# A Fourier mixer on one core: the setup and the first batch in another order, the fold of U on GpSimd, U's columns of the first batch in a pass of their own, and two of its four channel pieces moved into the loop

## The chip, the core and the metric

The kernel runs on one core of a Trainium2 chip. A core has five engines with a queue each, and every queue is worked in order: TensorE (PE; its weight loads are listed apart as PEld), VectorE (DVE), ScalarE (ACT), GpSimd (POOL) and SyncE (SP, which only issues transfers). The metric is the device time of one execution in microseconds (us); less is better. Times below that look like "at 47.2" are us from the first instruction of the profiled execution.

## The reference

`x` has shape 8 x 3136 x 256 (batch, sequence, channel) in float32. Without its casts the reference is:

```python
X = np.fft.fft(np.fft.fft(x, axis=1), axis=2).real   # along the sequence, then along the channels
h = X.transpose(0, 2, 1) @ U @ V                     # U 3136x32, V 32x3136
u = X + h.transpose(0, 2, 1)
out = u + np.maximum(u @ w_ch1, 0) @ w_ch2           # 256x1024 and 1024x256
```

So each batch has a two-dimensional Fourier transform of which the real part is kept, a low-rank mixing along the sequence, and a two-layer product over the channels. The last is most of the work: 49 chunks of 512 rows.

## The kernel before

**Tables.** The kernel makes its cosine and sine tables itself. `iota` on POOL gives the frequencies (`krow`, `kev`, `ncol`) and the row numbers for the gathers (`xidx`); DVE turns them into phases (`phase`, L180 and L182), ACT into sines (`sine`, L187; `cosine_even`, L604 and L606). By symmetry most of the tables follow from a quarter of them: `mirror_even` and `cosine_odd` copy with a sign on ACT, `other_even` and `other_odd` multiply by a row of alternating signs (`srow`) on DVE, and `halve` (L310, L312) halves one row with a scalar per partition. `TABE`, `TABO` and `TABS` hold the tables for even, odd and half-odd rows. `MSN` and `MC` are the sine and cosine of the channel transform; row 0 of `MSN` is overwritten with +1 and -1 by two memsets on POOL (`msr`, L687 and L688), so that it carries the two lone channels.

**U.** The low-rank factor U is transformed once. `fold_u` (L206 to L223) adds and subtracts forward rows `UF` and reversed rows `UR`; `transform_u(t)` gives three steps for t = 0 (sine) and t = 1 (cosine): `even_k` and `odd_k`, 36 small matmuls (L256) together, and `evict`, five ACT copies (L298 to L304) into spare columns of the tables. From then on, each group of matmuls of a batch's sequence transform also gives 32 columns of the product with U (`tab`).

**A batch.** `x` is loaded twice, forward by four indirect gathers on POOL (`load_f`, into `xf`) and reversed by SP (`load_r`, into `xr`); `load_0` brings the few rows that fall outside. DVE folds: `along_d` (L350 subtracts, L352 adds channels d and 256-d, in bf16), `alone` (the two channels without a partner), `mirror` (forward against reversed rows, L360 and L363), `half` (L368) and `fourth` (L372). The results `GO` and `GC` are the weights of the sequence transform. `seq(b, par, typ, pn)` is one group of matmuls (L427) for odd or even outputs (`par`), sine or cosine side (`typ`), first or second half (`pn`); the first half is copied to `ev` by ACT (L432) and for odd outputs turned into `eh` by DVE (L435, L437), and after the second half DVE joins both into `A` or `B` (L452 to L462). The join of the odd sine group is followed by a change of sign on POOL (L465). `chan(b, ch, h)` transforms one of four pieces along the channels for one of two halves (L473 with `MC`, L475 with `MSN`), and ACT copies it to `S` or `T` (L477). `lowrank` multiplies `tab` with `MDT` (L485) into `TA` and then makes a mirrored row of `VA` from `S` and `T` on DVE (L489). `VA` holds V in its first 32 rows, that mirrored row, and zeros.

**A chunk.** `front(c)` multiplies `TA` with `VA` (L511) and DVE adds it to `S` or `T`, giving `u` (L519); `first_product` multiplies with W1 (L531) and ACT applies the ReLU (L533); `second_product` multiplies with W2 (L547) and DVE adds `u` (L553 to L556) before the result is stored.

**What sets the order.** Up to `front(0)` the instructions of each engine run in the order in which the program lists them (`manual_schedule`, closed by `order.close()`). There the first batch is folded by columns: first all that the sine side needs (columns 0 to 128 and 256, 257), then the cosine side (128 to 256). A one-element transfer `gate` (L692) makes SP wait for batch 0's forward rows before it loads batch 1. After that a planner orders each engine's work; the listing gives its order of preference, and `due` spreads the steps of batch b (`transform(b)`: 8 fold steps, 8 groups, 8 channel pieces, `lowrank`) over the chunks of batch b-1.

Of the kernel before, what the change touches and what calls it, by code (L numbers as in the profile page):

```python
# [16 lines left out]
P = 128  # L17
PQ = 98
KP = PQ + 1
# [12 lines left out]
def kernel(  # L32
# [87 lines left out]
    load_0(x, xf, xr, 0, D)  # L120
    for q0 in (1, 0):
        load_r(x, xr, 0, q0, 2, D)
    iota(kev[:, 0:NT], [[-2, 2], [-4, NT // 2]], 392)
    iota(kev[:, NT:2 * NT], [[-2, NT]], 391)
# [40 lines left out]
    srow = cpool.tile([KP, 2 * NT], BF16, name="srow")  # L165
# [31 lines left out]
    phe = gen.tile([KP, 2, 2 * NT], I32, name="phe", bufs=1)  # L197
    uy = cpool.tile([KP, 2, 2, 2, NI * R], FP32, name="uy")
# [7 lines left out]
    def fold_u():  # L206
        for t in range(2):
            op = AL.add if t else AL.subtract
            nc.vector.tensor_tensor(uy[:, t, 0].rearrange("p a (i r) -> p a i r", r=R),
                                    UF[:, 0:4:2], UR[:, 3::-2, ::-1], op=op)  # L210
            nc.vector.tensor_tensor(uy[:, t, 1].rearrange("p a (i r) -> p a i r", r=R),
                                    UR[:, 0:4:2, ::-1], UF[:, 3::-2], op=op)
        nc.vector.tensor_tensor(GUO.rearrange("p t n i r -> p (t n) (i r)"),  # L213
                                uy.rearrange("p t n a x -> p (t n) a x")[:, :, 0],
                                uy.rearrange("p t n a x -> p (t n) a x")[:, :, 1], op=AL.subtract)
        nc.vector.tensor_tensor(ueven.rearrange("p t n x -> p (t n) x"),
                                uy.rearrange("p t n a x -> p (t n) a x")[:, :, 0],
                                uy.rearrange("p t n a x -> p (t n) a x")[:, :, 1], op=AL.add)
        for c in range(2):
            nc.vector.tensor_tensor(GUC[c].rearrange("p t i r -> p t (i r)"), ueven[:, :, 0],  # L220
                                    ueven[:, :, 1], op=AL.add if c == 0 else AL.subtract)
            nc.vector.tensor_single_scalar(NUC[c][:], GUC[c][:, :, 2, :], -1.0, op=AL.mult)
            nc.vector.tensor_single_scalar(NUO[:, :, c, :], GUO[:, :, c, 2 - 2 * c, :], -1.0, op=AL.mult)  # L223
# [27 lines left out]
    def transform_u(t):  # L251
# [22 lines left out]
        def even_k():  # L274
            pu = PU[t] = psum.tile([P, 16, R], FP32, tag="dft", name="pu", bufs=3)
# [49 lines left out]
    def cosine_odd(i):  # L325

        sgn = 1.0 if i == 0 else -1.0
        nc.scalar.activation(both(1, i, 1, 0, 1, NT), both(0, i, NT - 1, NT - 1, -1, NT),
                             AF.Copy, scale=sgn)
        nc.scalar.activation(TABO[1][:, 0, i // 2, 0:2 * NT], TABO[0][:, 0, i // 2, 2 * NT - 1::-1][:, 0:2 * NT],  # L330
                             AF.Copy, scale=sgn)

    def other_odd(t):

        nc.vector.tensor_tensor(TABO[t][:, 1, :, 0:2 * NT], TABO[1 - t][:, 0, :, 0:2 * NT],
                                strip(srow[:], 0, [[0, 2], [1, 2 * NT]]), op=AL.mult)

    def other_even(t):

        def cells(u, nm):  # L340
            v = TABS[u][:, nm, 0, :]
            return bass.AP(v.tensor, v.offset + off_t(u, 1),
                           [v.ap[0], [WS + off_t(u, 3) - off_t(u, 1), 2], [1, NT]])
        nc.vector.tensor_tensor(cells(t, 1), cells(1 - t, 0),
                                strip(srow[:], 0, [[0, 2], [1, NT]]), op=AL.mult)
# [8 lines left out]
    def alone(qs, src, dst):  # L354

        nc.gpsimd.tensor_copy(dst[:, qs, :, 128:257:128], src[:, qs, :, 0:129:128])
# [36 lines left out]
    def seq(b, par, typ, pn):  # L393
# [8 lines left out]
        d = ST[b]  # L402
        pt = psum.tile([P, QW], FP32, tag="dft", name="pt", bufs=3)
        mm = []

        def add(t, col, odd):

            if par == 0:
                for c in range(2):
                    g = GC[b % 2][0 if (c == 0) == (t == 1) else 1]  # L410
                    lo, hi, at = ((0, TE - NT + NE, 0), (TE - NT + NE, WE, TE - NT))[c]
                    for i in ((0, 2) if odd else (1, 3)):
                        mm.append((at, g[:kp(i), i, col:col + P], TABE[t][:kp(i), i, lo:hi]))
            else:
                for i in ((0, 2) if odd else (1, 3)):
                    at = 0 if odd else NT * slot(t, i)
                    tab = TABO[t] if odd else TABS[t]
                    for nm in range(2):
                        mm.append((at, GO[b % 2][:kp(i), nm, i, col:col + P],
                                   tab[:kp(i), nm, i // 2, :]))  # L420
        if typ == 1:
            add(1, 128, pn == 1)
        else:
            add(0, 0, pn == 1)
            add(1, 256, (pn == 1) == (par == 1))
        for n, (at, w, rhs) in enumerate(mm):
            nc.tensor.matmul(pt[:, at:at + rhs.shape[-1]], w, rhs, start=(n == 0),  # L427
                             stop=(n == len(mm) - 1), skip_group_check=True)
        if pn == 0:
            ev = d["ev"] = wp.tile([P, QW], FP32, tag="ev", name="ev", bufs=2)  # L430
            w = WO if par else QW
            nc.scalar.copy(ev[:, :w], pt[:, :w])  # L432
            if par == 1:
                eh = d["eh"] = wp.tile([P, 2 * NT], FP32, tag="eh", name="eh", bufs=2)
                nc.vector.tensor_tensor(eh[:, 0:NT], ev[:, NT - 1::-1], ev[:, WO - 1:WS - 1:-1],  # L435
                                        op=AL.subtract)
# [314 lines left out]
```

## Time and profile before

| what | value |
|---|---|
| median of 3 runs | 490.25 us (489.94 to 490.83) |
| the profiled execution's own time | 490.67 us |
| its span, first to last instruction | 488.9 us |
| PE busy | 449.7 us (92% of the span) |
| DVE busy | 342.7 us (70%) |
| ACT busy | 273.3 us (56%) |
| POOL busy | 88.1 us (18%) |
| HBM read and written | 29.26 MB and 25.69 MB |
| first matmul of U's transform | at 19.3 us |
| first group of batch 0 on PE | at 31.2 us |
| first channel piece of batch 0 | at 47.2 us |
| first `u` of chunk 0 on DVE | at 54.1 us |
| first group of batch 1 on PE | at 73.1 us |

Busy shares are averages over a beginning, in which the tables and the first batch are made, and a long loop. In the page's slices each digit is the busy share of one fortieth of the span in tenths. The chain of waits lists the work that ended last, followed back from the end; in order of time its lines give start, length, engine, what was written, and the line. A group of instructions is given with its shortest, median and longest duration in ns. A timeline line gives start, length, engine, line, operation, output and inputs with their shape, and in brackets how long the engine idled before and what released it.

### The profile page before, as it was taken

How to read it: one execution, taken by the hardware profiler on the slowest of the kernel's cores; microseconds unless marked ns; L12 is line 12 of the kernel's file. 1: busy time of each engine (PE TensorE's matmuls, PEld its weight loads, DVE VectorE, ACT ScalarE, POOL GpSimd, SP SyncE). 2: the span in 40 equal slices, each digit the busy share in tenths (PEclk: the TensorE clock that was granted, in tenths of full speed). 3: DMA queues.
4: the chain of work that ended last, by engine and by line, in shares of the span. 5: the costliest groups of instructions: out<-in, count | busy, mean ns of one | idle time of the engine just before them, and what ended most of it. 6: DMA issues, size and time to landing. Idle time of an engine off the chain costs nothing.

```text
span 488.9 us, 8177 instructions
## 1 busy us (share of the span) xinstructions
PE 449.7 (92%) x3096; PEld 299.9 (61%) x3096; DVE 342.7 (70%) x771; ACT 273.3 (56%) x533; POOL 88.1 (18%) x109
## 2 busy tenths in 40 slices
PE   0364799999999999999999999999999999999997
PEld 0342267666766666666766676666766676666665
DVE  5999699999999999997984358343743374434333
ACT  5331655665557554765566655756466556656562
POOL 7745230424144321610010001000010001000000
PEclk9997899999999999999999999999999999999999
DMA  5778389499839995595232422334223352333433
GB/s 149 157 135 236 64 152 254 134 253 260 231 89 220 245 249 163 134 272 142 70 104 65 131 67 68 102 89 129 67 66 86 108 88 86 88 98 99 128 90 126
DMA packets 87275, 67.14 MB, mean 137 GB/s; under 512 B 53920, under 2 KB 80556, under 8 KB 87236
## 3 DMA queue, kind: packets, MB, share of 16 engines
q1 hardware_dynamic: 81588, 51.86, 41.2%
q0 software_dynamic: 5648, 14.76, 11.8%
q8 instruction: 24, 0.39, 0.3%
q14 instruction: 15, 0.12, 0.1%
HBM read 29.26 MB, written 25.69 MB: 112 GB/s over the span
## 4 chain that ended last, share of the span: by engine, by line
PE 79%; DVE 16%; issue 2%; POOL 1%; ACT 1%; DVEq 0%; POOLq 0%
PE p L547 32%; PE p L531 31%; PE pt L427 6%; PE ph L511 4%; PE pst L473 3%; PE pst L475 2%; DVE eof L352 1%; DVE B L452 1%; DVE eof L350 1%; DVE u L519 1%; DVE eor L350 1%; DVE eor L352 1%; DVE A L452 1%; DVE B L456 1%; POOL uf L56 1%
## 5 line engine op out<-in xcount | busy, mean ns | idle before, releaser
L533 ACT ACTIVATE h<-p 128x512 bf16<-128x512 f32 x392 | 218.5, 597 | 139.6 <-PE p L531 139.4
L531 PE MATMUL p<-u,w 128*128 128x512 bf16 x784 | 210.1, 379 | 2.7 <-DVE u L519 2.7
L547 PE MATMUL p<-w,h 128*128 128x256 bf16 x1568 | 203.7, 273 | 0.0
L547 PEld LDWEIGHTS <-h 128*128 128x128 bf16 x1568 | 153.1, 98 | 59.2 <-DVE o L556 0.3
L531 PEld LDWEIGHTS <-w 128*128 128x128 bf16 x784 | 75.5, 98 | 59.8 <-issue 3.8
L553 DVE TENSOR_TENSOR o<-p,ut 128x4 f32<-128x4 f32 (+1 forms) x100 | 16.1, 161 | 111.3 <-PE p L547 111.2
L56 POOL DMA_INDIRECT xf<-in_x_dram,xidx x32 | 40.2, 1257 | 72.8 <-DVE eof L352 51.4
L465 POOL TENSOR_SCALAR B<-B 1x392 bf16<-1x392 bf16 x8 | 14.6, 1823 | 181.9 <-DVE tab L462 129.7
L556 DVE TENSOR_TENSOR o<-p,ut 128x254 f32<-128x254 f32 (+1 forms) x100 | 40.5, 405 | 0.0
L555 DVE TENSOR_TENSOR o<-p,ut 128x254 f32<-128x254 f32 (+1 forms) x100 | 40.5, 405 | 0.0
L519 DVE TENSOR_TENSOR u<-ph,S 128x512 bf16<-128x512 f32 (+15 forms) x64 | 34.9, 554 | 0.1
L432 ACT COPY ev<-pt 128x424 f32<-128x424 f32 (+1 forms) x32 | 16.4, 513 | 32.9 <-PE pt L427 21.4
L519 DVE TENSOR_TENSOR u<-ph,T 128x512 bf16<-128x512 f32 (+15 forms) x64 | 34.8, 553 | 0.0
L427 PEld LDWEIGHTS <-go 98*128 98x128 bf16 x192 | 19.4, 102 | 18.9 <-DVE go L368 7.1
L511 PE MATMUL ph<-va,ta 128*128 128x512 bf16 (+18 forms) x128 | 29.7, 329 | 0.5 <-ACT ta L488 0.5
L427 PE MATMUL pt<-te,gc 98*128 98x229 bf16 (+1 forms) x192 | 24.8, 268 | 0.3 <-DVE tab L459 0.2
L473 PE MATMUL pst<-A,mc 128*128 128x392 bf16 (+1 forms) x64 | 22.7, 355 | 2.3 <-DVE A L452 1.4
L427 PE MATMUL pt<-to,go 98*128 98x424 bf16 x96 | 21.8, 367 | 2.6 <-DVE tab L462 2.6
L475 PE MATMUL pst<-B,msn 128*128 128x392 bf16 (+1 forms) x64 | 22.7, 354 | 0.0
L427 PEld LDWEIGHTS <-gc 98*128 98x128 bf16 x192 | 18.6, 100 | 6.4 <-DVE tab L459 2.8
L477 ACT CAST S<-pst 128x392 bf16<-128x392 f32 (+1 forms) x32 | 15.7, 489 | 12.1 <-PE pst L475 12.1
L256 PE MATMUL pu<-guo,ts 99*98 99x32 bf16 (+1 forms) x16 | 2.3, 239 | 19.3 <-DVE guo L213 19.3
(120 smaller groups left out, 364.1 us busy)
## 6 DMA issues: line engine op xcount, KB each, us to landing
out_dram<-o SPq DMA_DIRECT2D x48, 512.0 KB
xr<-in_x_dram SPq DMA_DIRECT2D x7, 1568.0 KB
xr<-in_x_dram SPq DMA_DIRECT2D x2, 784.0 KB
ut<-u SPq DMA_TRANSPOSE x49
xf<-in_x_dram,xidx POOLq DMA_INDIRECT x32, 6.6
w<-in_moe_w_ch_dram POOLq DMA_DIRECT2D x1, 512.0 KB, 7.8
out_dram<-o SPq DMA_DIRECT2D x4, 128.0 KB
va<-in_moe_V_dram POOLq DMA_DIRECT2D x2, 196.0 KB, 5.2
```

Of the source, the lines that this page charges most:

```text
L56: nc.gpsimd.indirect_dma_start(out_, None, bass.AP(t.tensor, t.offset, [[w, rows], [1, w]]), bass.IndirectOffsetOnAxis(idx, 0), element_of ...
L427: nc.tensor.matmul(pt[:, at:at + rhs.shape[-1]], w, rhs, start=(n == 0), stop=(n == len(mm) - 1), skip_group_check=True)
L432: nc.scalar.copy(ev[:, :w], pt[:, :w])
L473: nc.tensor.matmul(pt[:, :hi - lo], MC[:, h * P:(h + 1) * P], d["A"][:, lo:hi], start=True, stop=False)
L475: nc.tensor.matmul(pt[:, :hi - lo], MSN[:, h * P:(h + 1) * P], d["B"][:, lo:hi], start=False, stop=True)
L511: nc.tensor.matmul(ph[:, col:col + hi - lo], TA[b % 2][:, s * P:(s + 1) * P], VA[b % 2][:, lo:hi], start=True, stop=True)
L519: nc.vector.tensor_tensor(u[:, s, col:col + hi - lo], ph[:, col:col + hi - lo], src, op=AL.add)
L531: nc.tensor.matmul(p1[:], W1[:, s, j * P:(j + 1) * P], k["u"][:, s, :], start=(s == 0), stop=(s == 1))
L533: nc.scalar.activation(k["h"][:, j, :], p1[:], AF.Relu)
L547: nc.tensor.matmul(p2[:, t % w, :], h[:, j, rs], W2[:, j, :], start=(j == 0), stop=(j == JT - 1))
L555: nc.vector.tensor_tensor(o[:, ts, 1:P], p2[:, :w, 1:P], ut[:, ts, 1:P], op=AL.add)
L556: nc.vector.tensor_tensor(o[:, ts, P + 1:D], p2[:, :w, P + 1:D], ut[:, tT, P - 1:0:-1], op=AL.add)
```

## The change

Only the part up to `front(0)` and the first steps of the loop change.

- **Transfers.** `kev` is made before the gathers. SP issues U's reversed rows and x's reversed rows first, then the outside rows of both. The gathers on POOL stay in their order. `gate` is gone. W1, W2 are issued on POOL behind `fold_u`; V is issued after the first batch's groups.
- **Tables.** `cosine_odd` moves from ACT to DVE; `other_odd` and `other_even` move from DVE to ACT, as two copies with a sign for every other column each. `srow` is gone.
- **U.** All twelve operations of `fold_u` move from DVE to POOL. The sine part of U's transform (`us`) runs before the forward folds of the first batch; its cosine part (`uc`) runs on PE between the odd and the even sine groups.
- **First batch.** The folds of the reversed rows precede U's transform; the others are listed so that each group of the sequence transform follows the folds that it needs: odd sine, even sine, odd cosine, even cosine. The lone channels (`alone`) are copied by ACT, those of `xf` behind `us[2]`, the sine evictions of U. `eh` of the odd sine group is made by POOL. `seq` is cut in two, with the second half's additions in `join`. For batch 0 the groups carry no U columns (`ne` is 0); `u_alone` computes them afterwards in 48 matmuls of 32 columns, and `lowrank` needs two matmuls instead of four.
- **Before the first chunk.** The zeros in the second buffers, the memsets of `VA` and `TA`, V's transfers and the memsets of row 0 of `MSN` stand on POOL behind the groups, in this order. Channel pieces 0 and 1 are computed, with the `T` half copied by DVE; pieces 2 and 3 and the mirrored row (`mirror_row`) are steps due in the first three slots of the loop.

The core of the diff, with lines that only rename or split left out:

```diff
+    iota(kev[:, 0:NT], [[-2, 2], [-4, NT // 2]], 392)
+    iota(kev[:, NT:2 * NT], [[-2, NT]], 391)
     nc.gpsimd.iota(xidx[:], pattern=[[S // 4, B], [S // 16, 4]], base=97, channel_multiplier=-1)
+    load_r(moe_U, UR, 0, 0, 4, R)
+    for q0 in (1, 0):
+        load_r(x, xr, 0, q0, 2, D)
     load_0(moe_U, UF, UR, 0, R)
-    load_r(moe_U, UR, 0, 0, 4, R)
+    load_0(x, xf, xr, 0, D)
     for q in range(4):
         load_f(moe_U, UF, 0, q, R)
...
     def fold_u():
         for t in range(2):
             op = AL.add if t else AL.subtract
-            nc.vector.tensor_tensor(uy[:, t, 0].rearrange("p a (i r) -> p a i r", r=R),
+            nc.gpsimd.tensor_tensor(uy[:, t, 0].rearrange("p a (i r) -> p a i r", r=R),
                                     UF[:, 0:4:2], UR[:, 3::-2, ::-1], op=op)
...
+    def u_alone(b, tag):
+        d = state(b)
+        pt = psum.tile([P, 2, R], FP32, tag=tag, name="ptu", bufs=BUFS[tag])
+        for typ in range(2):
+            mm = []
+            for t, col in ((1, P),) if typ else ((0, 0), (1, 256)):
...
+            for n, (w, rhs) in enumerate(mm):
+                nc.tensor.matmul(pt[:, typ, :], w, rhs, start=(n == 0), stop=(n == len(mm) - 1))
+        nc.scalar.copy(d["tab"][:, :, 0, :], pt[:])
...
+        if b == 0 and h == 1:
+            nc.vector.tensor_copy(d["T"][:, lo:hi], pt[:, :hi - lo])
...
+    for part in range(2):
+        along_d(OD, xr, EOR_, part)
     for i in (0, 2):
         cosine_odd(i)
     nc.vector.memset(lrow[:, 1, 0:1], 128.0)
     nc.vector.tensor_single_scalar(pcol[:], pcol[:], 1.0 / D, op=AL.mult)
     pd = gen.tile([P, 2 * P], I32, name="pd", bufs=1)
     phase(pd[:], lrow.rearrange("p a l -> p (a l)"), pcol[:], 17)
+    for part in range(2):
+        along_d(EV, xr, EOR_, part)
+    for t in range(2):
+        halve(t)
+    for t in range(2):
+        other_odd(t)
+    for t in range(2):
+        other_even(t)
+    alone(OD, xr, EOR_, nc.scalar.copy)
+    alone(EV, xr, EOR_, nc.scalar.copy)
     sine(MSN[:, 0:128], pd[:, 0:128], 17, -1)
     sine(MSN[:, 128:256], pd[:, 128:256], 17, 1)
     cosine(MC[:], pd[:], 17)
...
+    us, uc = transform_u(0), transform_u(1)
+    fold_u()
+    us[0]()
+    us[1]()
+    us[2]()
+    nc.gpsimd.dma_start(out=W1[:, 0, :], in_=moe_w_ch1[0:P, :])
+    gather(w1t[:], moe_w_ch1, D, pint[:], H, 0)
+    nc.gpsimd.dma_start(out=W2[:], in_=moe_w_ch2.rearrange("(j p) d -> p j d", p=P))
+    alone(EV, xf, EOF_, nc.scalar.copy)
+    alone(OD, xf, EOF_, nc.scalar.copy)
+    for part in range(2):
+        along_d(EV, xf, EOF_, part)
+    mirror(0, slice(0, 128), AL.subtract)
+    mirror(0, slice(128, 258), AL.add)
     along_d(OD, xf, EOF_, 0)
     mirror(1, slice(0, 128), AL.subtract)
     mirror(1, slice(256, 258), AL.add)
+    for cols in (slice(0, 128), slice(256, 258)):
+        half(0, 1, cols)
+    seq(0, 1, 0, 0, "dft", nc.gpsimd)
+    seq(0, 1, 0, 1, "dft")
+    sin_odd = dict(ST[0])
+    for cols in (slice(0, 128), slice(256, 258)):
+        half(0, 0, cols)
+        for c in range(2):
+            fourth(0, c, cols)
+    uc[0]()
+    uc[1]()
+    uc[2]()
+    seq(0, 0, 0, 0, "dft")
+    seq(0, 0, 0, 1, "p1")
+    sin_even = dict(ST[0])
     along_d(OD, xf, EOF_, 1)
     mirror(1, slice(128, 256), AL.add)
+    half(0, 1, slice(128, 256))
+    seq(0, 1, 1, 0, "p1")
+    seq(0, 1, 1, 1, "p1")
+    cos_odd = dict(ST[0])
+    join(0, 1, 0, sin_odd)
+    half(0, 0, slice(128, 256))
     for c in range(2):
         fourth(0, c, slice(128, 256))
+    join(0, 0, 0, sin_even)
+    seq(0, 0, 1, 0, "dft")
+    seq(0, 0, 1, 1, "dft")
+    join(0, 1, 1, cos_odd)
+    u_alone(0, "p2")
+    join(0, 0, 1)
+
+    zeros(nc.gpsimd, 1)
     for s in range(2):
+        nc.gpsimd.memset(VA[s][R:2 * R].bitcast(I32), 0)
+        nc.gpsimd.memset(VA[s][2 * R:P].bitcast(I32), 0)
+        nc.gpsimd.memset(TA[s][:], 0.0)
...
         nc.gpsimd.dma_start(out=VA[s][:R, :], in_=moe_V)
     nc.gpsimd.memset(msr[:, :, 0:1], 1.0)
     nc.gpsimd.memset(msr[:, :, 1:2], -1.0)
+
+    for ch in range(2):
+        for h in range(2):
+            chan(0, ch, h)
+    lowrank(0)
     nc.gpsimd.tensor_copy(W1[:, 1, :], w1t[:])
-
-    gate = cpool.tile([1, 2], FP32, name="gate")
-    nc.sync.dma_start(out=gate[:], in_=xf[0:1, 3, 0, 0:2])
     load_x(1)
...
+    due = {0: [lambda h=h: chan(0, 2, h) for h in range(2)],
+           1: [lambda h=h: chan(0, 3, h) for h in range(2)], 2: [lambda: mirror_row(0)]}
```

More of the change, by code (lines that the diff above doesn't have):

```diff
@@ L197 @@
     phe = gen.tile([KP, 2, 2 * NT], I32, name="phe", bufs=1)
+    nc.gpsimd.iota(pint[:], pattern=[[0, 1]], base=D, channel_multiplier=-1)
+    nc.gpsimd.memset(pint[0:1], P)
+    w1t = gen.tile([P, H], FP32, name="w1t", tag="w1t", bufs=1)
     uy = cpool.tile([KP, 2, 2, 2, NI * R], FP32, name="uy")
@@ L660 @@
+    mirror(0, slice(128, 258), AL.add)
     along_d(OD, xf, EOF_, 0)
-    alone(OD, xf, EOF_)
     mirror(1, slice(0, 128), AL.subtract)
     mirror(1, slice(256, 258), AL.add)
-    for par in (1, 0):
-        half(0, par, slice(0, 128))
-        half(0, par, slice(256, 258))
-    for c in range(2):
-        fourth(0, c, slice(0, 128))
-        fourth(0, c, slice(256, 258))
-    along_d(OD, xr, EOR_, 1)
-    along_d(EV, xf, EOF_, 1)
-    mirror(0, slice(128, 256), AL.add)
-    along_d(EV, xr, EOR_, 1)
+    for cols in (slice(0, 128), slice(256, 258)):
+        half(0, 1, cols)
```

206 lines of the change are left out of this document (89 added, 117 removed).

## The prediction, made before the changed kernel was run

> **What bounds the kernel now.** I read the page's slices first, then the chain of waits in order of time, then the timelines of VectorE (DVE), GpSimd (POOL) and TensorE (PE) over the first 60 us. The slices show PE full from the sixth slice (12.2 us each) on, and DVE nearly full from the second to the eleventh:
>
> ```profile
> PE   0364799999999999999999999999999999999997
> DVE  5999699999999999997984358343743374434333
> POOL 7745230424144321610010001000010001000000
> ```
>
> After 100 us PE is busy 384.3 of 388.9 us, and the edit leaves that work alone. So what counts is when the first chunk reaches the products, and how PE is fed just after. The chain in time (start, length, what):
>
> ```profile
> 12.40 3.85 DVE te L310 x2
> ...
> 32.78 1.12 DVE eor L352
> ...
> 46.24 0.91 DVE A L452
> 47.20 0.49 PE pst L473
> ...
> 53.08 0.93 DVE va L489
> ...
> 54.69 0.68 DVE u L519
> 55.37 1.12 DVE eof L350
> ```
>
> From 16 to 47 us DVE is the bound; then eight channel pieces on PE, then the first `u`. The marks to beat: first group on PE 31.2, channel pieces 47.2, first `u` 54.1. Three more readings carry the sum. The halving at L310, which costs 0.27 us at its first use, here:
>
> ```profile
> L310 DVE TENSOR_SCALAR te<-te,hv x2: 3657/3726/3794, 12.4 to 12.6; 99x197 bf16<-99x197 bf16 x1, 99x196 bf16<-99x196 bf16 x1
> ```
>
> and POOL meanwhile, instruction behind instruction until 16.3:
>
> ```profile
> 13.50 0.54 POOL L146 MEMSET go<- 99x504 int32 x1
> 13.97 0.57 POOL L148 MEMSET gc<- 99x252 int32 x2
> 14.46 1.42 POOL L639 MEMSET va<- 128x1568 int32 x1
> 15.81 0.32 POOL L640 MEMSET ta<- 128x256 bf16 x1
> ```
>
> The halving's input was ready (ACT's mirror ended at 12.4); it ended when POOL's stream did. A dense POOL stream can hold DVE. And the clock (us; PE, PEld, DVE, ACT, POOL busy; granted clock, DMA share, GB/s):
>
> ```profile
> 46.00:48.00 2.00, 0.80 (x3) 0.41 (x3) 2.00 (x6) 0.00 (x0) 0.00 (x0) 0.50 1.00 244
> 48.00:50.00 2.00, 2.00 (x8) 0.88 (x6) 0.05 (x3) 1.47 (x3) 0.00 (x0) 0.50 0.79 182
> ```
>
> The channel pieces ran at half clock, 0.33 us a matmul against 0.165 for the same ones at 91 us.
>
> **The change, step by step.** Times are us from the span's start.
>
> Edits with little on the path. `kev` ahead of the gathers ends DVE's 2.2 us wait at 7.9. SP issues x's reversed rows from about 1.1 instead of 5.15, so they land earlier. ACT loses 4 copies (0.52) and gets 8 sign copies (0.35 to 0.5). Without the gate, batch 1's reversed rows are issued when batch 0's have been read (before: 36.97). W1's and W2's transfers follow `fold_u` on POOL (5.0 of issue, from 22.4 before), landing near 40, wanted near 59. The 48 group matmuls lose 32 columns each, 0.013 at full clock: 0.6. Sine-odd's `eh` goes to POOL, two operations of 196 elements, 1.0 by step 1's price, wanted 9 later. All this gains little, because DVE's queue now has `lrow` and `pcol` ahead of the second reversed fold, and POOL makes these at 13.4, behind the same eight gathers as before.
>
> 1. `fold_u` on POOL. Its queue is free at 13.4 plus `pint` 0.23; U's last gather was issued at 6.28 and landed 7.9 later. Start 14.2. It is 12 instructions with 2,816 elements a partition (4x256, 2x512, 2x256, 4x64); on DVE they took 17.09 to 21.2. No two-input operation on POOL is in the trace. Below: the cast of 128x1024 in 1.03, 1.0 ns an element, and 0.09 fixed each (the 1x1 memset): 3.9. Above: the 1x392 sign flip in 1.29, 3.3 ns: 10.4. I take two inputs as twice the one-input cast, 2.0 ns: 6.8, end 21.0. The Trainium skill (GPSIMD Engine Reference, 3.1 Elementwise) measured an addition of 2,048 floats at 4,497 ns on this engine; by that estimate the end would be about 0.6 later; no row here shows it.
>
> 2. DVE beside it. From 13.4: the phase of the channel tables 1.1, the second reversed fold 2 x 1.13, six halvings 1.7: end 18.5 if nothing holds it; if the POOL stream holds all of it as at L310, 21.0 + 0.6 + 2.3 + 1.7 = 25.6. L310 is the same instruction, and a two-input one fared alike: the mirror and its two-column rest took 1.80 at 28.70, beside POOL's 1.03 cast, against 0.78 for the like pair at 25.64. So I let the two streams add up, 13.4 + 5.1 + 6.8 = 25.3, and take 25.0, as a part may fall before the stream begins. The Trainium skill (SBUF — State Buffer, Who interferes with whom) has an exclusive lock between the two engines, for two-input operations against POOL's reads and for two-port scalar operations; by that the streams add up too. L310's 3.79 and the mirror's 1.80 agree that one of them waits whole instructions.
>
> 3. `other_even` on ACT waits for the halvings, and U's sine pass on PE reads it: 25.6, and 36 matmuls at 0.083 (the pitch from 23 to 26): 28.6. Five evictions 1.1 (23.92 to 24.94): 29.7. Now the lone columns of `xf` are copied on ACT *behind* these evictions: 30.0. DVE, done with the even `xf` folds and one mirror at 28.0, waits for them. That wait is new.
>
> 4. DVE to the first group: mirror 0.7, fold 1.13, mirrors 0.8, half 0.75: first group at 33.4 (before 31.2), although the second parts of the folds no longer precede it.
>
> 5. PE then runs in one line: sine-odd 8 x 0.163 and 8 x 0.327 at the half-speed pitch of the same groups at 31 to 35 (3.9), U's cosine pass 3.0, sine-even 16 x 0.10, cosine-odd's first four 0.4. DVE has its folds done at +4.1, but the next instruction in its queue is cosine-odd's `eh`, which waits for PE and for ACT's 0.5 copy; the first join is queued behind it. `eh` 0.55 and join 0.96 end 11.0 after the first group: 44.4.
>
> 6. The tail on POOL. The sign flip waits for that join. Behind it, in this order: flip 1.3, `zeros` 1.1, four memsets of VA 5.5 (1.41 each, overlapping a little), TA 1.0, two V transfers 1.2, and only then the two memsets of row 0 of MSN 0.4, which every channel piece reads. 10.5, so 54.9. Beside it DVE's other joins (0.6 + 0.8 + 1.7 + 1.0 + 1.7 = 5.8) end at 50.2, and U's columns apart (48 matmuls at 0.1, the weight-load row of 98 ns) behind cosine-even (3.0 after the join) at 52.2. So POOL is last by 2.7; it covers the 4.8 of U's pass, which would otherwise be last itself. Before, these memsets were done at 29.
>
> 7. Four channel pieces, 8 matmuls, 0.165 to 0.33 each (PE idles 2.7 ahead of them): 2.0. Low rank, TA and `ph` to `u` 1.6 as at 52.5 to 54.1; the mirror row, 0.96, leaves this stretch but lay beside them. First `u` 58.5: 4.4 later than before.
>
> 8. The loop. PE gets 8 matmuls x 0.165 = 1.3 more, DVE one mirror row 0.96 and two T copies of 0.5. DVE was full from 54 to 75, PE idled 2.7 between 54 and 70, so part is hidden. Batch 1's four gathers on POOL now follow W1's cast and end near 61 (before 35.9 to 43.5); landing 5.5 to 11 later, against 52 before. Least: -1.5, if the delayed folds leave DVE to `u`; most: +6. I take +1.5.
>
> Sum: the profiled execution took 490.67 (span 488.9); +4.4 + 1.5 gives 496.6. It stood 0.42 above the median, so I forecast 496.1.
>
> **Rivals.**
> A, faster: POOL adds at the cast's price and does not hold DVE. `fold_u` ends at 18.1, the halvings at 18.5, the lone columns 23.5, first group 26.9; with steps 5 to 7 unchanged (25.1 from first group to `u`) the first `u` is at 52.0, 2.1 earlier, and with nothing lost in the loop 488.2. For it: the two halvings at 9.85 took 0.59 together beside POOL's gathers, hardly held. Against: L310 and the mirror. It decides when the first group starts before 27.5 (29.0 for `u` alone).
> B, much slower: batch 1's rows are late in earnest. The first group of batch 1 ran at 73.1, right behind the fold of its data at 72.2, with DVE full since 54. Its rows landed at 52, before they were wanted; now the second even quarter is issued near 58.5 and lands at 64 or later, where 59.7 would do. Some 4.5 more: 500.6. Against: batch 1's last channel pieces, at 100, had 4 us to spare before chunk 6.
> C, the tail is shorter: VA's memsets now cover 32 and 64 partitions, not 128. If that price goes by partitions they take 2.1 instead of 5.5 and U's pass at 52.2 ends last: 2.7 less, 493.4. No row shows two heights of one memset; a 1x128 memset took 0.24, which speaks against it.
>
> **How the numbers follow.** Forecast 0.47 (own range 493.5 to 499.5), B 0.23, A 0.17, C 0.13. A change under 0.2%, some 1 us, can't be told from none. A gives faster; C reaches into no change for a small part; the rest is slower: 0.17, 0.05, 0.78. The range goes from just above A (489; a third of A's chance lies above that) to B with a part of the upper price of step 1 (3.6 more): 502. The likeliest is 496.1.
>
> **What would show it.** Step 1: twelve POOL instructions of about 0.6 from 14 to 21. Step 2: `halve` or the reversed folds far above 0.27 and 1.2. Step 3: DVE waiting for ACT's lone columns before a mirror. Step 5: DVE idle some 5 us before `eh`. Step 6: PE or its weight load at the first channel pieces waiting for POOL's `msn` memset; if they wait for DVE's A or for nothing, step 6 is wrong. Step 8: L350 of batch 1 waiting for the `xf` transfer. Most would fall if POOL's tail started much earlier than 43, or if the order of the loop, planned anew, fed PE better than before.

## The result, and the profile after

The changed kernel takes 502.58 us (median of 4 runs, 500.38 to 503.57), the kernel before beside it 490.27 (489.94 to 490.83). The ratio is 1.0244, with a 95% interval of 1.0209 to 1.0279: the change makes the kernel 2.4% slower. The forecast was slower by 5.8 us; it is slower by 12.3.

The profiled execution is the quickest of the four, 500.38 us with a span of 498.6. Its marks against those of before:

| mark | before | forecast | after |
|---|---|---|---|
| first group of batch 0 on PE | 31.21 | 33.4 | 33.55 |
| first join (odd sine) ends on DVE | 42.6 | 44.4 | 43.2 |
| last memset of MSN's row 0 ends | 29 | 54.9 | 54.4 |
| first `u` | 54.08 | 58.5 | 58.54 |
| second chunk's first `u` | 59.79 | | 67.87 |
| batch 1's first group | 73.12 | | 82.54 |
| end of the span | 488.9 | 494.8 | 498.6 |

The four stretches sum to the whole: +4.46 to the first `u`, +3.62 from there to the second chunk's, +1.34 to batch 1's first group, +0.28 from there to the end, 9.70 in all. The medians differ by 2.6 more, because before's profiled execution stood 0.40 above its median, and after's 2.20 below its own (the section on surprises has what shows of that).

The page's slices of the changed kernel, 12.5 us each. PE is emptier in the second, third, fifth and sixth and then as full as before; DVE, before at nine from the second slice on but for the fifth, now isn't from the third to the sixth:

```profile
PE   0056579999999999999999999999999999999997
DVE  5976379999999989998886347434634365343343
POOL 7955832333217341350010000100010001000000
```

The chain of waits of the changed kernel (start, length, what), where before it had DVE's `A`, channel pieces and `u`:

```profile
58.17 4.96 DMA xf<-in_x_dram,xidx
63.13 2.46 issue
65.58 1.23 DVE eof L353
...
66.83 1.01 DVE va L529
...
67.87 0.70 DVE u L559
...
68.62 1.01 PE p L571 x2
```

A gather of batch 1's rows has got into the chain; before, no transfer stood there. The second chunk's `u` waits behind a fold of batch 1 (L353) and behind the deferred mirrored row (`va`). The profile has the gather landed at 63.13 and names nothing for the 2.46 us after it. That the fold waits for these rows is a reading: POOL's copy of the same rows' lone columns starts at the same moment, 65.61, and the wait is gone in the run that loads the rows early.

The timelines of POOL, DVE and PE in the changed kernel (start, length, engine, line, operation; in brackets idle time and releaser), one fence each:

```profile
18.75 2.11 POOL L215 TENSOR_TENSOR guo<-uy 99x512 bf16<-99x512 f32 x1
20.83 1.26 POOL L218 TENSOR_TENSOR ueven<-uy 99x512 f32<-99x512 f32 x1
...
45.96 1.40 POOL L730 MEMSET va<- 32x1568 int32 x1
47.39 1.41 POOL L731 MEMSET va<- 64x1568 int32 x1
...
54.14 0.23 POOL L737 MEMSET msn<- 1x128 bf16 x1
54.30 1.03 POOL L743 CAST w<-w1t 128x1024 bf16<-128x1024 f32 x1
...
58.17 0.95 POOL L56 DMA_INDIRECT xf<-in_x_dram,xidx  x1 [0.31 <-issue]
```

```profile
19.67 2.48 DVE L312 TENSOR_SCALAR te<-te,hv 99x197 bf16<-99x197 bf16 x2
...
30.22 0.70 DVE L363 TENSOR_TENSOR eos<-eof,eor 99x1040 bf16<-99x1040 bf16 x1 [3.45 <-ACT eof L359]
...
65.58 1.22 DVE L353 TENSOR_TENSOR eof<-xf 99x1016 bf16<-99x1016 f32 x1 [2.46 <-issue]
```

```profile
39.11 1.54 PE L429 MATMUL pt<-te,gc 98*128 98x197 bf16 x16
...
48.44 0.49 PE L509 MATMUL pst<-A,mc 128*128 128x393 bf16 x1 [1.15 <-DVE A L468]
54.43 0.51 PE L511 MATMUL pst<-B,msn 128*128 128x393 bf16 x1 [5.50 <-POOL msn L737]
...
68.62 1.01 PE L571 MATMUL p<-u,w 128*128 128x512 bf16 x2 [2.78 <-DVE u L559]
```

POOL's tail is one line of work: after MSN's memsets the cast of W1, then the four gathers at 55.53, 56.87, 58.17 and 59.42. PE pays for it twice: 5.50 us between the two matmuls of the first channel piece, and 2.78 in the second chunk. Before, that second idle stretch was 1.25, at 60.53.

### The profile page after: what moved, and what is told of

The parts are those of the page before. It is cut to its first block, busy times and chain, and to the rows that moved or that the text cites. A ratio compares the mean times of both kernels' runs of the same rounds, so it can differ in the third digit from the quotient of the medians.

```text
span 498.6 us, 8214 instructions
## 1 busy us (share of the span) xinstructions
PE 445.5 (89%) x3087; PEld 299.2 (60%) x3142; DVE 339.9 (68%) x754; ACT 273.0 (55%) x538; POOL 110.4 (22%) x121
## 4 chain that ended last, share of the span: by engine, by line
PE 78%; DVE 7%; issue 2%; DMA 1%; ACT 0%; DVEq 0%; ACTq 0%
PE p L587 32%; PE p L571 31%; PE pt L429 7%; PE ph L551 4%; PE pst L509 2%; PE pst L511 2%; DMA xf<-in_x_dram,xidx 1%; PE ptt L523 1%; DVE A L468 1%; DVE u L559 1%; DVE eor L353 1%; DVE A L470 1%; DVE eor L355 1%; DVE B L468 1%; DVE eof L353 0%
## 5 line engine op out<-in xcount | busy, mean ns | idle before, releaser
L571 PE MATMUL p<-u,w 128*128 128x512 bf16 x734 | 203.1, 381 | 5.9 <-DVE u L559 3.7
L480 POOL TENSOR_SCALAR B<-B 1x392 bf16<-1x392 bf16 x8 | 11.4, 1422 | 193.6 <-DVE tab L477 136.0
L56 POOL DMA_INDIRECT xf<-in_x_dram,xidx x32 | 44.2, 1380 | 45.2 <-DVE eof L355 31.7
L445 ACT COPY ev<-pt 128x425 f32<-128x425 f32 (+3 forms) x32 | 16.4, 511 | 29.4 <-PE pt L429 25.1
L551 PE MATMUL ph<-va,ta 128*128 128x512 bf16 (+14 forms) x123 | 28.4, 327 | 0.8 <-ACT ta L525 0.5
L429 PE MATMUL pt<-te,gc 98*128 98x229 bf16 (+2 forms) x192 | 24.4, 265 | 3.4 <-DVE gc L375 2.9
L353 DVE TENSOR_TENSOR eor<-xr 99x1016 bf16<-99x1016 f32 x16 | 20.1, 1254 | 5.0 <-DMA xr<-in_x_dram 5.0
L258 PE MATMUL pu<-guo,ts 99*98 99x32 bf16 (+1 forms) x16 | 2.0, 222 | 23.9 <-DVE ts L314 22.4
```

Source lines behind the costliest of these rows:

```text
L56: nc.gpsimd.indirect_dma_start(out_, None, bass.AP(t.tensor, t.offset, [[w, rows], [1, w]]), bass.IndirectOffsetOnAxis(idx, 0), element_of ...
L353: nc.vector.tensor_tensor(dst[:, qs, :, 1:128], lo, hi, op=AL.subtract)
L551: nc.tensor.matmul(ph[:, col:col + hi - lo], TA[b % 2][:, s * P:(s + 1) * P], VA[b % 2][:, lo:hi], start=True, stop=True)
L571: nc.tensor.matmul(p1[:], W1[:, s, j * P:(j + 1) * P], k["u"][:, s, :], start=(s == 0), stop=(s == 1))
```

## The experiments

Each is an edit of the changed kernel unless it says otherwise. Times are medians, beside 489.7 to 490.1 for the kernel before on the same chips. Two theories stood against each other at the outset: that the late end of POOL's tail and the late rows of batch 1 each cost their own time and can be cured one by one, or that either hides behind the other.

**MSN's memsets early.**

```diff
     nc.gpsimd.dma_start(out=W2[:], ...)
+    nc.gpsimd.memset(msr[:, :, 0:1], 1.0)      # both taken from the end of the tail
+    nc.gpsimd.memset(msr[:, :, 1:2], -1.0)
```

> The two memsets of row 0 of MSN stand on POOL right behind W2's transfer instead of behind VA, TA and V; nothing else is changed. Theory of terms that add up (the prediction's): the channel pieces start at 48.4 instead of 54.4, V's transfer for the first buffer (issued at 49.3, landing about 3 to 5 later) is the next to set the first u, at 53 to 55, and the total falls by about 4, to 498.5. Rival (the rows of batch 1 set the pace): the four gathers still follow W1's cast on POOL, 0.4 earlier, land near 65, and the second chunk's u still waits behind batch 1's fold in DVE's queue, at 67 to 68; the total falls by less than 1, to about 502.

503.79 us, ratio 1.0280 (1.0230 to 1.0329): nothing gained, as the rival had it. The wait for MSN is gone, the channel pieces run through from 51.29 (later than the 48.44 above, because PE ran at a slower pitch in this execution; see the last section), and two other waits have taken its place. DVE's timeline of this run:

```profile
57.91 0.69 DVE L559 TENSOR_TENSOR u<-ph,S 128x512 bf16<-128x512 f32 x1 [3.23 <-POOL w L743]
...
67.22 1.22 DVE L353 TENSOR_TENSOR eof<-xf 99x1016 bf16<-99x1016 f32 x1 [5.78 <-issue]
...
70.43 0.68 DVE L559 TENSOR_TENSOR u<-ph,S 128x512 bf16<-128x512 f32 x1
```

The first `u` now waits 3.23 for the cast of W1, which still ends POOL's tail. It doesn't read W1. By the listing, `u` is allocated after the setup's memory was given back (`setup.close()`), and what this cast still has to read there is `w1t`; that it is this memory is argued, not shown. Where the cast stands earlier (the tail taken apart, below), the first `u` waits for PE alone. And the fold of batch 1 waits 5.78 for rows, where it waited 2.46.

**Batch 1's rows early.**

```diff
     cos_odd = dict(ST[0])
+    load_x(1)            # was behind the cast of W1, ahead of setup.close()
     join(0, 1, 0, sin_odd)
```

> Batch 1's rows are asked for ahead of the first join: the four gathers run on POOL from about 38 to 43, in a gap, and land by 50 instead of 65; nothing else is changed. Theory (the late rows cost the loop what the prediction under-sized): the first u stays at 58.5, the second chunk's u comes at 63 to 64 instead of 67.9, and the total falls by 3.5 to 5, to 497.5 to 499. Rival (the loop's loss is the extra work in it, eight matmuls, two copies and the mirror row): the total stays within 1 of 502.5.

501.05, ratio 1.0235 (1.0218 to 1.0252). From the first to the second chunk's `u` it takes 6.7 (61.04 to 67.74) instead of 9.3, so step 8's missing 2.6 is there. DVE's timeline has the fold of batch 1 without a wait:

```profile
62.24 1.21 DVE L353 TENSOR_TENSOR eof<-xf 99x1016 bf16<-99x1016 f32 x1
...
67.74 0.69 DVE L559 TENSOR_TENSOR u<-ph,S 128x512 bf16<-128x512 f32 x1
```

In the median 1.5 of it is left, between what the theory and the rival had, and the profiled execution ends only 0.1 earlier than the changed kernel's: it ran at the slower pitch, which puts its first `u` 2.5 later. MSN's memsets still hold the channel pieces, until 56.92.

**Both together**, the two edits above in one kernel.

> Both of the moves before, the row 0 memsets and batch 1's rows. Theory (two waits, each hides the other's gain): first u at 53 to 55, second chunk's u at 59 to 60, total 491 to 494, that is 8 to 11 below the change and more than the two single gains together. Rival (gains add up): the sum of the two single gains, whatever they are.

496.08, ratio 1.0133 (1.0116 to 1.0150): 6.5 less than the changed kernel, where the single edits gave -1.2 and +1.5. First `u` 57.64, second chunk's 64.30, batch 1's first group 78.85. So the two waits hide each other, and the additive theory falls. The gain stops short of the 491 to 494 that I had expected: the first `u` waits 3.25 for the cast of W1, as above.

**`fold_u` back on DVE.**

```diff
-            nc.gpsimd.tensor_tensor(uy[:, t, 0]...      # and so for all twelve
+            nc.vector.tensor_tensor(uy[:, t, 0]...
```

> fold_u back on DVE, everything else as changed. Theory (the fold on POOL and what it does to DVE is on the path): the halvings cost 0.27 each, U's sine pass ends near 25.5 instead of 28.9, the mirror that waits for the lone columns starts near 27 instead of 30.2, and all later marks, POOL's tail and the gathers included, come 3 earlier: total about 499.5. Rival (POOL's tail or the rows have slack over this path): below 1 of change.

501.32, ratio 1.0243 (1.0218 to 1.0268). In the profiled execution (497.47) every mark is 2.6 to 2.9 earlier: first group 30.77, first `u` 55.92, second chunk's 64.96, batch 1's group 79.63. The medians differ by 1.3 only, with runs from 497.5 to 502.4, so the 2.9 rests on two profiled executions at the same pitch.

**PE kept busy before the first group.** Thirteen matmuls that nobody reads, between U's sine pass and the first group.

```diff
     us[1]()
+    fl = psum.tile([P, QW], FP32, tag="p1", name="fl", bufs=3)
+    for n in range(13):
+        nc.tensor.matmul(fl[:, 0:2 * NT], TABO[0][:PQ, 0, 0, 0:P], TABO[0][:PQ, 0, 0, 0:2 * NT], ...)
```

> Thirteen idle matmuls of 392 columns, whose result is not used, are added to the changed kernel on PE between U's sine pass and the first group, into a PSUM buffer that is free then; the output is the same. Theory (the spread of the change, 500.4 to 503.6, and some 2 to 3 of its loss are PE's clock: in the executions seen, U's cosine pass and the even sine group behind the idle stretch ran either at 0.047 and 0.094 a matmul or at 0.083 and 0.164): with PE kept busy from 29 to 33 the odd sine group runs at 0.163 instead of 0.327 for 392 columns, the first join ends near 41 instead of 43.2 or 46.2, the total falls by about 4 to 498.5 and the runs lie within 1 of each other. Rival (the clock is not what makes the difference, or the fill only delays the first group): total 502 or more, the same spread.

501.11, ratio 1.0208 (1.0155 to 1.0260), runs of 503.0, 503.5, 499.2 and 498.2. In the profiled one PE is busy from 27 to 45 with 0.33 us idle in all, and still takes 0.33 for 392 columns, 0.163 for 197. That enough work on PE always brings the quicker pitch (below) falls with this execution; how PE ran in the two quicker ones isn't recorded.

**Nothing deferred.** All four channel pieces and the mirrored row ahead of the first chunk, `due = {}`, every copy to `T` on ACT.

```diff
...
-    for ch in range(2):
+    for ch in range(4):
         for h in range(2):
             chan(0, ch, h)
     lowrank(0)
+    mirror_row(0)
...
-    due = {0: [lambda h=h: chan(0, 2, h) for h in range(2)],
-           1: [lambda h=h: chan(0, 3, h) for h in range(2)], 2: [lambda: mirror_row(0)]}
+    due = {}
```

> The deferral alone is undone: all four channel pieces are computed before the first chunk, copied by ACT, and the mirror row with them. Theory (the deferred work is not hidden in the loop: two copies and the mirror row, 2.0 on a DVE that is full there, and 1.3 on PE): first u 1.3 to 2.6 later, but the second chunk's u no later than 68 since it waits for batch 1's rows either way, and from there to batch 1's first group 13.3 as before the change instead of 14.7: total 1 to 2.5 lower. Rival (deferring pays what it takes off the beginning): total 1.5 to 2.5 higher.

503.29, ratio 1.0279 (1.0257 to 1.0301). Against the run with the thirteen matmuls, whose pitch was the same: first `u` 64.32 for 61.89, second chunk's 69.30 for 70.47, batch 1's first group 85.07 for 85.14. Here putting the two pieces off neither costs nor saves, and neither theory's total came.

**The tail taken apart.** Rows early as above; the cast of W1 behind the odd-sine `eh`; MSN's memsets and the first halves of VA, TA and V behind W2's transfer; `zeros` and the second halves behind the first join.

```diff
     nc.gpsimd.dma_start(out=W2[:], ...)
+    nc.gpsimd.memset(msr[:, :, 0:1], 1.0)
+    nc.gpsimd.memset(msr[:, :, 1:2], -1.0)
+    for s in (0,):       # VA, TA and V of this s
...
     seq(0, 1, 0, 0, "dft", nc.gpsimd)
+    nc.gpsimd.tensor_copy(W1[:, 1, :], w1t[:])
...
     cos_odd = dict(ST[0])
+    load_x(1)
     join(0, 1, 0, sin_odd)
+    zeros(nc.gpsimd, 1)
+    for s in (1,):       # VA, TA and V of this s
```

> The changed kernel with POOL's list in another order: row 0 of MSN and the first buffers' VA, TA and V right behind W2's transfer, W1's cast behind the odd sine eh, batch 1's rows before the first join, the second buffers behind it. Theory (POOL's order costs the beginning twice, by the channel pieces' wait and by the late rows, and a third wait on W1's cast, whose buffer the first u reuses, kept the earlier experiment's first u at 57.6): channel pieces at 48.4 or 51 by PE's clock, first u at 52.6 to 55, total 492 to 494.5. Rival (something else holds the first u at 57 to 58): total 496 as with both moves.

495.58, ratio 1.0118 (1.0098 to 1.0138); the profiled execution took 491.89. Its first `u` is at 52.71, earlier than before's, the second chunk's at 59.38, batch 1's group at 74.06. The marks are those of the theory; the median lies nearer to the rival's total, for the other three executions took 494.9 to 496.6.

**The tail all early, `fold_u` on DVE, the first join ahead of the cosine-odd group.** All of POOL's memsets between W2's transfer and `eh`, W1's cast as in the last run. `load_x(1)` keeps its place in the listing; as the join has moved up, batch 1's rows now follow the first join, here and in the two runs built on this one (the expectation of the first of them says before).

```diff
     nc.gpsimd.dma_start(out=W2[:], ...)
+    for s in (0,):       # VA, TA and V of this s
+    zeros(nc.gpsimd, 1)
+    for s in (1,):       # VA, TA and V of this s
+    nc.gpsimd.memset(msr[:, :, 0:1], 1.0)
+    nc.gpsimd.memset(msr[:, :, 1:2], -1.0)
...
+    join(0, 1, 0, sin_odd)
     seq(0, 1, 1, 0, "p1")
     seq(0, 1, 1, 1, "p1")
     cos_odd = dict(ST[0])
-    join(0, 1, 0, sin_odd)
+    load_x(1)
```

> As the last, with fold_u on DVE, all of POOL's memsets between W2's transfer and the odd sine eh, and the first join ahead of the odd cosine group. Theory: first group at 30.8, channel pieces near 45.5 to 48, first u at 50 to 52.5; the loop still pays the deferred work, some 2.5: total 488 to 491, about the kernel before. Rival (the groups' new order is itself slower, whatever POOL does): first u later than 54, total above 492.

492.32, ratio 1.0033 (1.0006 to 1.0060): the first `u` is at 52.32, as the theory had it, the total as the rival had it. The first join now runs at 35.91 without a wait. What waits is cosine-odd's `eh`, 5.09 us, and U's cosine pass stands in front of its group: it is on PE from 34.97 to 37.98.

**U's cosine pass into PE's idle time.** The changed kernel with one move; its evictions go behind ACT's lone columns.

```diff
     us[1]()
+    uc[0]()              # was between the odd and the even sine groups
+    uc[1]()
     us[2]()
```

> The changed kernel with one move: the 36 matmuls of U's cosine pass stand on PE behind the sine pass, in the time in which PE idles before the first group, and its five evictions on ACT behind the lone columns. Theory (PE's line from the first group to the first join sets the marks, and this pass is 1.7 to 3.0 of it): DVE waits 2 to 3 us less before the cosine-odd eh, and the first join, GpSimd's tail, msn's memsets, the first u and batch 1's gathers all come 1.7 to 3.0 earlier; total 1.7 to 3.0 below the changed kernel, 499.5 to 501. Rival (the join waits for GpSimd's eh or for ACT, or GpSimd's tail for something else): the marks after the first join stay, total within 0.7 of 502.6. The pitch of the small matmuls (0.083 or 0.047) may come out either way, as it did in the other runs; 2.6 us hang on it.

499.11, ratio 1.0198 (1.0182 to 1.0214), 3.5 below the changed kernel and somewhat more than expected. The four runs lie within 1.6 us. Not all of the 3.5 need be the pass itself: against the changed kernel's profiled execution, which was at the quicker pitch, the end comes 1.3 earlier and the first `u` 0.85.

**All of these moves**: the tail all early, `fold_u` on DVE, the first join ahead, U's cosine pass early.

> All five moves together: batch 1's rows loaded before the first join, W1's cast behind the odd-sine eh, all of GpSimd's memsets and the two of msn between W2's transfer and that eh, fold_u on DVE, the first join ahead of the cosine-odd group (these were the kernel at 492.3), and U's cosine pass ahead of the first group as well. There eh waited 5.1 us, 3.0 of them for U's cosine pass. Theory: first join and all marks 2 to 3 earlier, first u near 50, total 489.3 to 490.5, no different from the kernel before or a little faster. Rival (the first chunk's lead is eaten by batch 1's folds on a full DVE): first u earlier, batch 1's first group where it was, total 491.5 to 493.

488.69, ratio 0.9977 (0.9965 to 0.9988): a little faster than the kernel before, by 0.23%. Timelines of PE and DVE in this run:

```profile
31.69 1.49 PE L429 MATMUL pt<-ts,go 98*128 98x196 bf16 x8 [1.56 <-DVE go L371]
...
45.16 0.49 PE L509 MATMUL pst<-A,mc 128*128 128x393 bf16 x1 [1.39 <-DVE A L468]
45.44 0.54 PE L511 MATMUL pst<-B,msn 128*128 128x393 bf16 x1
```

```profile
49.52 0.69 DVE L559 TENSOR_TENSOR u<-ph,S 128x512 bf16<-128x512 f32 x1 [0.98 <-PE ph L551]
...
56.19 0.69 DVE L559 TENSOR_TENSOR u<-ph,S 128x512 bf16<-128x512 f32 x1
```

The first channel piece runs without a wait for MSN, and the first `u` is 4.56 ahead of before's. Of that lead 0.96 is gone by the second chunk's `u` (6.67 apart, before 5.71), 1.35 more by batch 1's first group at 70.87, and the span ends 2.0 earlier. DVE is busy 15.94 of the 16 us from 52 to 68 here, with the deferred work and batch 1's folds, so it has no idle time that would keep the lead.

**The same with nothing deferred**, with the edit shown above for that.

> The kernel that measured 488.69 (all five moves and U's cosine pass ahead of the first group), now with all four channel pieces and the mirrored row computed before the first chunk and every copy to T on ACT. That kernel's first u stood 4.6 earlier than before's and its end only 2.0: it took 6.7 from the first to the second chunk's u where before took 5.7, and 14.7 from there to batch 1's first group where before took 13.3. If the deferred pieces, their copies and the mirrored row on a full DVE take the lead away: first u 1.3 to 2.5 later, the two stretches back at 5.7 and 13.3, total 487.5 to 488.5. If they are neutral, as in the changed kernel: total within 0.7 of 488.7. If the pieces were well hidden in the loop: 489.5 to 490.5.

488.37, ratio 0.9975 (0.9964 to 0.9985). First `u` 50.16, second chunk's 53.62, batch 1's group 69.41. Against the run above the medians differ by 0.3 and the ranges (487.1 to 489.7 and 487.3 to 489.2) overlap. The total fits two of the three expectations. The marks speak for the first: the first `u` is only 0.64 later, and from there to batch 1's first group it takes 19.25, as before the change (19.04), where the run above took 21.35. But this profiled execution is the quickest of its eight; in the medians undoing the deferral is neutral again.

**`fold_u` on POOL, alone, in the kernel before.** The opposite way round: nothing of the change but these twelve instructions.

```diff
-            nc.vector.tensor_tensor(uy[:, t, 0]...      # and so for all twelve
+            nc.gpsimd.tensor_tensor(uy[:, t, 0]...
```

> The kernel before with one part of the change: the twelve operations of fold_u on GpSimd in place of DVE, nothing else. They stand there ahead of the memsets. Theory (the two engines hold each other, and GpSimd takes two to three times DVE's 4.1 us): fold_u ends near 27 instead of 21.2, U's first matmuls start some 6 later, the folds of batch 0 on DVE, 4.1 shorter in number, are held as long; first group between 31 and 33.5, total 489.5 to 493. Rival (the two work side by side): DVE is 4.1 ahead, first group near 27.5 to 29, total 486 to 488.5.

495.41, ratio 1.0114 (1.0098 to 1.0129): 5.6 slower, and more than I had allowed. The timelines of POOL and DVE:

```profile
13.39 0.74 POOL L209 TENSOR_TENSOR uy<-uf,ur 99x256 f32<-99x256 f32 x1
...
20.11 2.23 POOL L216 TENSOR_TENSOR ueven<-uy 99x512 f32<-99x512 f32 x1
...
27.65 1.41 POOL L639 MEMSET va<- 128x1568 int32 x1
...
31.86 0.40 POOL L356 CAST eof<-xf 99x16 bf16<-99x16 f32 x2
```

```profile
17.30 3.92 DVE L350 TENSOR_TENSOR eor<-xr 99x1016 bf16<-99x1016 f32 x2
21.14 2.27 DVE L350 TENSOR_TENSOR eof<-xf 99x1016 bf16<-99x1016 f32 x1
...
32.14 0.17 DVE L360 TENSOR_TENSOR eos<-eof,eor 99x16 bf16<-99x16 bf16 x1 [7.59 <-POOL eof L356]
```

The twelve instructions take from 13.39 to 26.6 on POOL, 13.2 us (1.09 of it a wait for U's rows) where DVE needed 4.1. Meanwhile DVE's two folds of the reversed rows need 3.92 (before 2.35) and one forward fold 2.27 (before 1.20): the engines hold each other, in both directions. And what I had missed: POOL copies the lone columns in the kernel before, its memsets stand ahead of the last of them, and DVE idles 7.59 for it.

## Why the prediction was right in direction and short in size

**Steps 1 and 2: right in kind, step 1 too cheap.** The twelve folds took 14.81 to 27.3, not 14.2 to 21.0: 0.73 to 0.78 each for 256 elements, 2.9 to 3.0 ns an element where I took 2.0, and up to 1.69 for 256 and 2.11 for 512 where DVE's two-input folds ran beside. Beside the halvings it was DVE that was held: L312's first two took 2.48, POOL's 512 elements meanwhile 1.26. DVE was done with the halvings at 23.3, not 25.0; the two halves of the second reversed fold took 1.74 and 1.73. U's sine pass on PE ended at 29.0 for the forecast 28.6, so the sum hardly felt it. That is luck: POOL was 6.3 later than forecast, but PE had started on the first results at 22.4, where the step let its whole pass begin behind the sign copies. Rival A falls with it. The Trainium skill (SBUF — State Buffer, Who interferes with whom) describes an exclusive lock between the two engines; these stretched instructions on both sides agree.

**Steps 3 to 7: the right waits, sizes that cancel.** The lone columns behind U's evictions hold the mirror, as step 3 said (the 3.45 above, until 30.22 where I had 30.0). First group 33.55 for 33.4. The first join ended 1.2 before step 5's time, and the tail took 11.1 where step 6 had 10.5; so MSN's memsets end at 54.4 for 54.9, and PE waits for just these. From there to the first `u` it took 4.2, not 3.6. That the first `u` is within 0.1 is therefore partly luck. In the profiles at the slower pitch step 5's 11.0 from first group to join is 12.6 (MSN's memsets early), in this one 9.7. Step 6's two-sided doubt is settled too: a memset of 1,568 elements takes 1.40 on 32 partitions, 1.41 on 64 and 1.42 on 128, so rival C falls. U's 48 matmuls were over-priced at 4.8: they take about 1.5, but lay under the tail in any case.

**Step 8: the term that failed.** "I take +1.5" measured +5.2 in the profiled execution (3.62 + 1.34 + 0.28). That is 3.7 of the 6.5 by which the forecast of the slowdown fell short; 2.6 more lie between the profiled executions and the medians (the next paragraph). The mechanism was on the page as rival B, late rows at "some 4.5 more". I gave it too little weight for a reason that doesn't bear on it: batch 1's spare 4 us at its last channel pieces help a late transform, but the rows are wanted by an *instruction in DVE's queue ahead of the second chunk's `u`*, and what waits there holds the chunk. Moving the load alone brought the stretch between the two chunks from 9.3 to 6.7, and with all of the tail moved as well it stayed at 6.7 (before the change 5.7). Of the other 2.6, the deferred work on a full DVE can be 2.0: 1.03 for two copies to `T` and 1.01 for the mirrored row. In the medians it isn't saved by doing it earlier (503.29 for 502.58, 488.37 for 488.69), for then part of it lies in front of the first `u`. The prediction also misread the slices of before: DVE stands at nine not up to the eleventh but, from the sixth on, up to the eighteenth, some 220 us, so the loop had little idle DVE time to hide work in.

**Not in the sum at all: PE's pitch.** Step 5 took U's cosine pass at 3.0 and the sine-even group at 0.10 a matmul, one at the slow pitch and one at the fast. The profiles with the pass between the groups do both at one or both at the other; that is worth 2.9 us at the first channel piece. It would account for the median standing 2.2 above the profiled execution, but the other three executions left no timeline, so this isn't shown (below).

**Where the change loses, in sum.** Not in one part. `fold_u` on POOL costs 2.9 in the profiled executions, the order of POOL's tail and the place of batch 1's load together 6.5 to 7.0 in the medians, U's cosine pass between the groups 3.5 in the medians and 1.3 in the profiled executions; undoing or moving all of them, with the first join ahead of the cosine-odd group, turns +12.3 into -1.1. These prices come from different starting points and need not add up. So what is left of the rebuilt beginning in the kernel at 488.69 (folds of the reversed rows first, groups in order of their folds, U's columns apart, sign copies on ACT) beats the old one by 1.1; which of these gains it, no run shows.

## What to carry to other kernels

When a block of "free" work is moved to the end of a queue, list everything that queue feeds behind it, and every buffer that is given back only when it is done; two late feeds of one consumer hide each other, so move them together before judging either. A wait that a transfer puts on an instruction of the *next* batch is paid by this batch as soon as the instruction stands ahead in an in-order queue: ask what is queued behind, not how much slack the data has. Work moved from the bounding engine to GpSimd isn't off the path if that engine then runs beside it: here twelve instructions went from 4.1 us to 13.2 and stretched DVE's folds as well.

## What the runs showed of the hardware that I had not expected

**Nearly one program, two pitches.** In the profiles of the changed kernel and of the runs with `fold_u` on DVE and with the tail taken apart, PE does the 16 sine-even matmuls at about 0.086 each and U's cosine pass at 0.047. In those with MSN's memsets early, the rows early, both, thirteen more matmuls, nothing deferred, and all of the tail early, it takes 0.163 and 0.083, though the code on PE up to there is the same or nearly so. Where U's cosine pass stands early, it changes from one to the other within the sine-even group or right behind it. Sine-even with MSN's memsets early (PE's timeline, to be held against the 1.54 at 39.11 above):

```profile
40.37 2.80 PE L429 MATMUL pt<-te,gc 98*128 98x197 bf16 x16
```

and two of its windows (us; PE, PEld, DVE, ACT, POOL busy; granted clock, DMA share, GB/s):

```profile
39.00:42.00 3.00, 3.00 (x30) 2.86 (x29) 0.00 (x0) 1.13 (x6) 0.00 (x0) 1.00 0.12 23
...
51.00:54.00 3.00, 2.71 (x9) 1.00 (x8) 1.69 (x4) 0.98 (x2) 2.88 (x6) 1.00 0.27 33
```

The granted clock reads 1.00 in both, with matmuls at twice their time: here the pitch of the matmuls has to be read, not that column. The first channel piece starts at 51.29 in this run and at 48.44 in the changed kernel's profile, though their first groups start within 0.1 us. The unprofiled executions can't be looked into, but some kernels of this kind spread in two clumps (`fold_u` on DVE: 497.5 and 500.4 to 502.4; the tail all early: 488.4 twice and 491.4 to 494.2), and the kernel before doesn't (489.1 to 490.8 over all runs). With the tail all early the two quick executions list a mean granted clock of 0.992 and the eight others 0.999 to 1.000, so there the lower figure goes with the quicker execution; in the changed kernel it doesn't (503.57 lists 0.983). What decides the pitch stays open. The Trainium skill (TensorE: Matmul & The Clock Gate, Part 1) has the clock at half until some 3.4 us of sustained work, in a free-running window and variable from run to run; the changed kernel's profile agrees (slow from 33.55, fast from about 37.4), the run with thirteen matmuls does not, with 18 us of work at the slow pitch, nor do the others at that pitch, with PE busy for some 11 us in a row from the first group on.

**A memset's price didn't depend on the partitions**: 1.40, 1.41 and 1.42 us for 1,568 elements on 32, 64 and 128, against 0.51 for 504 elements on 99.

**Small matmuls took longer with 98 columns of weights than with 128.** At the slow pitch a matmul of 32 columns took 0.083 with 98 columns of weights (U's pass) and 0.028 with 128 (U's columns apart, 46 intervals from 45.80 to 47.08 in the changed kernel). The single weight loads there go the same way: 0.20 for 98 columns at 26.40, 0.10 for 128 at 47.11. That the columns make the difference is only argued: the two passes also swap which operand is the weight, and no run changed the columns alone.

**Gathers landed sooner without the reversed rows' load beside them.** Batch 1's four took 3.9 to 7.3 us from issue to landing in the changed kernel, where before it was 9.7 to 10.8, beside that load; that the load is the cause is argued. It didn't help, for they were issued some 20 us later.
